# One fp32 copy of p for all batches, and a new order of all steps, in a fused attention and token-mixing kernel

## The chip, the cores and the metric

The kernel runs on one core of a Trainium2 chip. The metric is the device time of one execution in microseconds (us). Before the change three runs gave 105.6, 106.25 and 106.4 us; the median is 106.25 us. One execution was also taken with the hardware profiler: 105.87 us of device time, of which 103.7 us are the span that the trace covers.

Engines: PE is TensorE (PEld its weight loads), DVE is VectorE, ACT is ScalarE, POOL is GpSimd, SP is SyncE, which here only issues transfers. A transfer that POOL issues is a software transfer (it can convert fp32 to bf16 on the way); one that SP or ACT issues is a hardware transfer (no conversion).

## The reference

Eight batches, eight heads, 576 rows, 64 columns per head, 32 pack rows.

```python
def sm_attn(qq, kk, vv):                 # softmax(qq kk^T / 8) vv
    ...
p_packed = sm_attn(p, k, v)              # 32 rows per head
out = sm_attn(q, p_packed, p_packed)     # 576 rows per head
x = out.transpose(0, 2, 1, 3).reshape(B, S, H * D)      # 576 x 512 per batch
wq, wk = x @ w_q, x @ w_k                                # 576 x 64 each
W_tok = scale * einsum('bsd,btd->bst', wq, wk)
mixed = einsum('bst,btd->bsd', W_tok, x)
return maximum(mixed, 0) @ w_out                         # 576 x 512 per batch
```

q, k and v are 9.4 MB each in fp32, p is 0.52 MB, w_out 1.05 MB, w_q and w_k 0.13 MB each, and the output is 9.4 MB.

## The kernel before

The kernel is one list of steps, ORDER (lines 12 to 56), worked through from left to right. Each word is one step: a name, its batch and part, `@` the engine, and `=` the PSUM banks. Every engine takes its own steps strictly in this order, so the list sets the order on PE, DVE, ACT, POOL and SP alike, and a step that waits holds all later ones of its engine. Nothing is rescheduled.

Per batch the steps are these. LD.k, LD.v, LD.q load k, v and q through POOL's software queue as bf16 into four rotating buffers each. KT transposes k on DVE in blocks (line 242 is the helper of all DVE transposes). S1 is the first score product on PE. X1 is its exponential on ACT. For batches 2 to 7 TE turns the result on DVE. PV is the product with v. RC and PP divide, on DVE; PT transposes the packed rows. QK multiplies them with w_k and w_q; QKE and QD copy that out of PSUM. QV transposes q on DVE. S2 is the second score product, in two or three parts, X2 its exponential on ACT, RS the row sums and RR the reciprocals on DVE (for batch 5 HA on POOL adds halves first, line 394). AM multiplies by the reciprocals, on DVE or POOL (line 411). AT transposes that on PE, AE copies it out. WKQ, WE, GM, GE, Y, YE, MX and MR are the token mixing, RL, RLR and RLF the ReLU copies, OT and OH the product with w_out (lines 546 and 583), OE, OEF, OEH its copies out of PSUM. ST, STF and STH store the output. LD.O loads w_out; LD.W0 and LD.W1 load w_k and w_q.

WARM steps (line 621) are matmuls on zeros. Their count is in units of 128 columns. They take PE's place in line like any other step.

HOLD.v7 (line 578) is a tiny transfer on SP's queue that reads the last v buffer. It waits until v of batch 7 has landed, and SP's stores stand behind it.

The software queue keeps at most eight transfers open: each load waits until the eighth one before it has landed (v of one batch counts as two).

The start works like this. For batches 0 and 1 (DIAG, line 9), S1 takes a block-diagonal copy of p, `pblk`, as its moving operand. Its source is loaded by itself: LD.E0 and LD.E1 (line 164) bring p of batches 0 and 1 in fp32 by hardware transfers, in pieces of 64 numbers, into `p32`; EC casts them on ACT, EX transposes them in blocks on DVE into `pe`, and four PB copies on DVE put the blocks into `pblk` (line 259). LD.H on SP's queue brings the first half of k of batch 0 in fp32, which HC casts on ACT; LD.g on POOL's queue brings the other half as bf16. p of all batches comes a second time: LD.P3, P2, P1 and P0 (line 160) are four software transfers of 32 rows each into `pbf`, and PX (line 254) transposes all of it into `pT` in one DVE instruction. S1 of batches 2 to 7 takes p from `pT`.

Of the kernel before, what the change touches and what calls it, by code (L numbers as in the profile page):

```python
# [22 lines left out]
RR.1.0@V WARM.7=0 PV.2.0=0,1 PV.2.1 RL.0.1@A RS.1.2@V AM.1.0@V QD.1@A MR.0=6,7 RLR.0@A LD.k4 RR.1.2@V
MX.0.0=2,3 LD.q3 RC.2@V AT.1.0=4 AM.1.2@V AT.1.2=5 AE.1.2@A RL.0.0@A PP.2.1@V AM.1.1@P AT.1.1=6 AE.1.1@A
PP.2.0@V AE.1.0@V WARM.2=7 WKQ.1.0=0,1 WKQ.1.2 WARM.2=7 WKQ.1.1 QV.2.2@V WE.1.0@A PT.2@V S2.2.3=4,5 S2.2.2=2,3
KT.3.2@V WE.1.1@A GM.1=7 QK.2=6 GE.1@V WARM.3=0 Y.1=0,1 X2.2.2@A QKE.2@V S1.3=2,3,6,7 X2.2.3@A RS.2.4@V
RR.2.4@V LD.v4 X1.3.1@A TE.3.1@V X1.3.0@A TE.3.0@V OT.0.0=4,5 OT.0.1 LD.q4 YE.1@A AM.2.2@V OT.0.2=6,7 OE.0.0@V
OT.0.3 MR.1=2,3 OE.0.1@A RLR.1@V MX.1.1=0,1 PV.3.0=4,5 PV.3.1 RL.1.1@A RC.3@V PP.3.1@V PP.3.0@V KT.4.2@V
AM.2.3@P QD.2@P AT.2.3=2 AE.2.3@A OT.1.4=3 MX.1.0=6,7 AT.2.2=5 OEF.1.4@A AE.2.2@V WKQ.2.0=0,1 PT.3@V QV.3.2@V
WKQ.2.1 RL.1.0@A WKQ.2.2 WE.2.2@A S1.4=2,3,4,5 X1.4.1@A X1.4.0@A TE.4.1@V OT.1.0=6,7 LD.k5 GM.2=0 QK.3=1  # L30
QKE.3@A S2.3.2=4,5 X2.3.2@A S2.3.3=2,3 X2.3.3@A GE.2@V Y.2=0,1 OT.1.1 OE.1.0@A TE.4.0@V YE.2@V PV.4.0=4,5
PV.4.1 MX.2.0=0,1 RL.2.0@A RS.3.4@V LD.v5 RR.3.4@V RC.4@V LD.q5 PP.4.1@V PP.4.0@V PT.4@V OT.1.2=2,3 OT.1.3
QK.4=6 QV.4.2@V MX.2.1=0,1 MR.2=4,5 OE.1.1@A RL.2.1@A RLR.2@V AM.3.3@P QKE.4@V AT.3.3=7 AE.3.3@V QD.3@P
S2.4.2=2,3 X2.4.2@A LD.k6 KT.5.2@V S2.4.3=4,5 OT.2.2=0,1 X2.4.3@A QD.4@V RS.4.4@V RR.4.4@V AM.3.2@P AT.3.2=6
WKQ.3.0=2,3 WKQ.3.1 AE.3.2@A LD.v6 WKQ.3.2 WE.3.2@A S1.5=4,5,6,7 OT.2.3 X1.5.1@A TE.5.1@V GM.3=2 GE.3@V
OT.2.0=6,7 LD.q6 X1.5.0@A Y.3=4,5 TE.5.0@V PV.5.0=2,3 PV.5.1 OE.2.1@A YE.3@V MX.3.0=0,1 AM.4.2@P RC.5@V
PP.5.0@V AM.4.3@P PP.5.1@V RL.3.0@A MX.3.1=4,5 RL.3.1@V LD.k7 QV.5.2@V OT.2.1 OE.2.0@A LD.v7 AT.4.2=2 AE.4.2@A
# [5 lines left out]
OE.3.1@A ST.3.1 OT.4.1 OE.4.0@A QK.6=6 QKE.6@A S1.7=2,3,0,1 RS.6.4@V AM.5.3@P AT.5.3=7 OT.4.2=4,5 AM.5.2@P
QD.5@P RR.6.4@V X1.7.1@A ST.3.4 X1.7.0@A AE.5.3@V TE.7.0@V AT.5.2=6 AE.5.2@A AM.6.3@P QD.6@P TE.7.1@V ST.2.0@P
WKQ.5.0=0,1 WKQ.5.1 WKQ.5.2 WE.5.2@A OT.4.3 OE.4.1@A ST.4.1 AT.6.3=7 QV.7.1@V AE.6.3@V GM.5=2 PV.7.0=0,1
PV.7.1 QV.7.0@V AM.6.2@P GE.5@A Y.5=4,5 RC.7@V AT.6.2=3 PP.7.0@V ST.1.0 WKQ.6.0=6,7 WKQ.6.1 AE.6.2@A YE.5@A
PP.7.1@V PT.7@V WKQ.6.2 MR.5=2,3 ST.3.0 MX.5.1=4,5 RLR.5@V WE.6.2@A RL.5.1@V S2.7.0=0,1 X2.7.0@A MX.5.0=2,3
# [607 lines left out]
```

## Time and profile before

| what | value |
|---|---|
| runs | 105.6, 106.25, 106.4 us |
| profiled execution | 105.87 us, span 103.7 us |
| PE busy | 97.0 us, of which line 621 (WARM) 23.75 us |
| DVE, ACT, POOL busy | 75.7, 66.2, 49.5 us |
| read from and written to memory | 30.28 MB and 9.44 MB |
| first S1, batch 0 | 8.29 us |
| first product with w_out | 38.45 us |
| v of batch 7 landed (HOLD goes) | 76.25 us |
| last matmul ends | 99.46 us |

The profile page gives busy time per engine, the span in 40 slices, the DMA queues, the chain of work that ended last, and the costliest groups. The timeline lists instructions of one engine in order of time: start, length, engine, line, operation, operands, and in brackets the idle time before it with what released it. GB/s counts bytes written, so a load that converts fp32 to bf16 reads twice what it shows.

### The profile page before, as it was taken

To read this page: it belongs to the slowest core of one execution; us is meant where nothing else is said; L and a number is where in the kernel's file an instruction comes from. 1 tells how busy PE (TensorE), PEld (TensorE's weight loads), DVE (VectorE), ACT (ScalarE), POOL (GpSimd) and SP (SyncE) were. 2 spreads that over 40 slices of the span, in tenths; PEclk is the share of its full clock that TensorE was granted. 3 is DMA by queue.
4 is the path that set the end of the run, shared out by engine and by line. 5 is a ranking of instruction groups with operands and counts; after the bars stand their busy time and mean duration, and the time that the engine had idled before them with its cause. 6 is when DMAs were issued, how large, how long until landed. Compare 5 with 4: busy or idle time off the path is not lost.

```text
span 103.7 us, 3603 instructions
## 1 busy us (share of the span) xinstructions
PE 97.0 (94%) x1544; PEld 58.6 (57%) x1544; DVE 75.7 (73%) x151; ACT 66.2 (64%) x109; POOL 49.5 (48%) x75
## 2 busy tenths in 40 slices
PE   5999999999999999799999999999999999999930
PEld 3897645666656644456546655683567654744420
DVE  5090382969899799798699979989988998616210
ACT  5243104246896864779869869898997796658430
POOL 5999372952163326920059599405689038000000
PEclk9999999999999999999999999999999999999996
DMA  3999999999999999999999999999999999999883
GB/s 108 238 180 186 202 210 200 211 210 212 209 211 209 206 208 214 212 210 205 213 212 207 216 208 207 215 210 205 210 251 344 396 398 400 402 409 403 330 315 115
DMA packets 14079, 25.16 MB, mean 243 GB/s; under 512 B 2160, under 2 KB 7024, under 8 KB 14064
## 3 DMA queue, kind: packets, MB, share of 16 engines
q0 software_dynamic: 10448, 16.88, 84.7%
q1 hardware_dynamic: 3200, 7.87, 19.9%
q8 instruction: 12, 0.20, 0.7%
q10 hardware_dynamic: 416, 0.20, 0.7%
q14 instruction: 3, 0.02, 0.1%
HBM read 30.28 MB, written 9.44 MB: 383 GB/s over the span
## 4 chain that ended last, share of the span: by engine, by line
PE 81%; DVE 9%; ACT 3%; POOL 2%; issue 1%; DVEq 0%; POOLq 0%; ACTq 0%
PE ps L546 25%; PE ps L621 19%; PE ps L321 6%; PE ps L379 5%; PE ps L452 4%; PE ps L498 3%; PE ps L425 3%; DVE rs L400 3%; PE ps L447 3%; PE ps L473 3%; PE ps L278 2%; PE ps L342 2%; PE ps L288 2%; POOL a L411 2%; DVE a L411 2%; ACT e L384 2%
## 5 line engine op out<-in xcount | busy, mean ns | idle before, releaser
L546 PE MATMUL ps<-wout,relu 128*128 128x512 bf16 x124 | 30.5, 380 | 0.0
L621 PE MATMUL ps<-o 128*128 128x128 f32 (+3 forms) x76 | 23.7, 455 | 1.3 <-DVE o L134 1.2
L411 POOL TENSOR_TENSOR a<-e,rr 128x1024 bf16<-128x1024 f32 (+2 forms) x13 | 15.6, 1212 | 19.1 <-DVE rr L405 10.5
L127 ACT ACTIVATE o<-ps 128x1024 f32<-128x1024 f32 (+2 forms) x17 | 15.0, 888 | 7.0 <-PE ps L546 6.4
L546 PEld LDWEIGHTS <-relu 128*128 128x128 bf16 x124 | 10.7, 98 | 12.4 <-issue 1.8
L621 PEld LDWEIGHTS ps<-o 128*128 128x128 f32 x76 | 12.9, 224 | 7.2 <-issue 4.9
L384 ACT ACTIVATE e<-ps 128x256 f32<-128x256 f32 (+2 forms) x19 | 11.3, 621 | 6.0 <-PE ps L379 5.6
L509 ACT ACTIVATE relu<-ps 128x1024 bf16<-128x1024 f32 (+1 forms) x14 | 12.7, 932 | 2.2 <-PE ps L498 1.1
L176 POOL DMA_DIRECT2D v_sb<-in_v_dram x16 | 10.1, 636 | 7.3 <-DMA q_sb<-in_q_dram 2.1
L242 DVE STREAM_TRANSPOSE kT<-k_sb 128x1152 uint32<-128x1152 uint32 (+1 forms) x9 | 11.0, 1225 | 3.0 <-DMA k_sb<-in_k_dram 3.0
L242 DVE STREAM_TRANSPOSE qT<-q_sb 128x1152 uint32<-128x1152 uint32 (+1 forms) x10 | 11.2, 1121 | 0.4 <-DMA q_sb<-in_q_dram 0.3
L400 DVE TENSOR_REDUCE rs<-e 128x16 f32<-128x512 f32 (+2 forms) x13 | 10.9, 845 | 0.4 <-ACT e L384 0.4
L321 PE MATMUL ps<-v_sb,e 64*64 64x192 bf16 x288 | 7.6, 245 | 0.6 <-DVE o L131 0.6
L299 ACT ACTIVATE e1T<-ps 128x576 bf16<-128x576 f32 x12 | 7.2, 662 | 1.3 <-PE ps L288 1.2
L127 ACT ACTIVATE aT<-ps 128x128 bf16<-128x128 f32 (+2 forms) x11 | 5.3, 506 | 3.5 <-PE ps L425 2.1
L321 PEld LDWEIGHTS <-e 64*64 64x64 bf16 x288 | 6.1, 106 | 2.5 <-issue 0.8
L127 ACT ACTIVATE wkq<-ps 128x448 bf16<-128x448 f32 (+1 forms) x9 | 6.3, 713 | 1.7 <-PE ps L452 1.4
L452 PE MATMUL ps<-aT,pqk 128*128 128x256 bf16 (+1 forms) x48 | 6.8, 246 | 0.1
L379 PEld LDWEIGHTS <-qT 64*128 64x128 bf16 x320 | 5.5, 94 | 2.3 <-issue 0.7
L379 PE MATMUL ps<-ppT,qT 64*128 64x64 bf16 x320 | 6.6, 190 | 0.0
L179 POOL DMA_DIRECT2D k_sb<-in_k_dram x7 | 5.2, 743 | 3.0 <-ACT pqk L127 3.0
L447 PE MATMUL ps<-pqk,aT 128*128 128x64 bf16 x80 | 6.1, 194 | 0.1
(79 smaller groups left out, 142.8 us busy)
## 6 DMA issues: line engine op xcount, KB each, us to landing
v_sb<-in_v_dram POOLq DMA_DIRECT2D x16, 288.0 KB, 11.9
out_dram<-o SPq DMA_DIRECT2D x9, 512.0 KB, 6.9
k_sb<-in_k_dram POOLq DMA_DIRECT2D x7, 576.0 KB, 12.1
q_sb<-in_q_dram POOLq DMA_DIRECT2D x6, 576.0 KB, 15.3
out_dram<-o POOLq DMA_DIRECT2D x4, 512.0 KB, 7.6
out_dram<-o SPq DMA_DIRECT2D x5, 256.0 KB, 3.3
q_sb<-in_q_dram POOLq DMA_DIRECT2D x4, 288.0 KB, 11.1
out_dram<-orem SPq DMA_DIRECT2D x4, 256.0 KB, 5.6
```

Source lines behind the costliest of these rows:

```text
L127: nc.scalar.activation(o, i, COPY)
L176: nc.gpsimd.dma_start(v_bufs[b % NL][halves(i), 0:7:2], src)
L242: nc.vector.transpose(o, i)
L321: nc.tensor.matmul(T["pv", b][halves(cc), i], lhsT, rhs, start=n == 0, stop=n == R - 1, skip_group_check=True)
L379: nc.tensor.matmul(ps[:, y, t - t0, i], lhsT, rhs, start=e == 0, stop=e == 1)
L384: nc.scalar.activation(e2[:, t0:t1].rearrange("a t (i y n) -> a y (t i) n", i=2, y=2), T["s2", b, c].rearrange("a y t i n -> a y (t i) n") ...
L400: nc.vector.tensor_reduce(rs[:, t0 * H:t1 * H], src, axis=AX, op=ADD)
L411: e.tensor_tensor(a2[:, t0:t1].rearrange("a t i (u l) -> a (t i u) l", l=L), e2v(b, c), T["rr", b][:, t0 * H:t1 * H].to_broadcast((P, (t1 ...
L452: nc.tensor.matmul(o, pqk[:, i, Dl:], aT[:, i, c0:c1], start=i == 0, stop=i == 1)
L509: nc.scalar.activation(o, i, RELU)
L546: nc.tensor.matmul(ps, lhsT, wout[:, j, :], start=j == 0, stop=j == NJ - 1)
L621: nc.tensor.matmul(bank(int(bk), [w]), warm[:, 0:P], rhs, start=True, stop=True)
```

## The change

p is loaded once. LD.N0 (on ACT's queue) and LD.N1 (on SP's, behind LD.H) bring half of the heads each, for all batches, in fp32, into `p32`. NC.0 on ACT and NC.1 on DVE cast them to bf16. PX is split in two halves, and now runs before the first S1. PB copies the blocks for batches 0 and 1 out of `pT`. LD.E0, E1, P0 to P3, EC and EX are gone. ORDER is new from end to end, on every engine.

```diff
 ORDER = """
-SET.warm@V SET.v0@V SET.pz0@V LD.E0@A SET.tab@A SET.aT1@V LD.H@S LD.P3 LD.E1@S EC@A EX@V PB.0.1@V LD.g0
-HC@A PB.0.3@V PB.0.2@V PB.0.0@V KT.0.0@V KT.0.1@V LD.v0 WARM.4=0 WARM.16.128=0 S1.0=0,1,2 X1.0.0@A WARM.6=3
-PV.0.0=4,5 PV.0.1 RC.0@V LD.q0 LD.P2 LD.r0 LD.W0 SET.mask@P LD.k1 SET.idf@V SET.aT0@V QV.0.1@V PP.0.0@V PP.0.1@V PT.0@V
-SET.v2@V QV.0.0@V WARM.15=3 S2.0.2=6,7 LD.W1 SET.v3@P SET.aT2@V LD.P1 KT.1.2@V S2.0.1=0,1 X2.0.1@A RS.0.1@V
-SET.v1@P S2.0.0=2,3 X2.0.0@A LD.v1 LD.P0 WARM.8=4 QK.0=4 RR.0.1@V AM.0.1@V QKE.0@A LD.q1 RS.0.0@V SET.aff@P
-SET.idb@V WARM.3=5 S1.1=0,1,2 X1.1.0@A WARM.6=5 PV.1.0=4,5 PV.1.1 X2.0.2@A RR.0.0@V AT.0.1=3 AM.0.0@V AT.0.0=2
...
-AT.4.3=3 AE.4.3@A LD.r7 OT.3.0=0,1 MR.3=4,5 RLR.3@A LD.q7 OT.3.1 KT.6.2@V OE.3.0@A WKQ.4.0=6,7 WKQ.4.1 PT.5@V
...
+LD.H@S SET.warm@V SET.v0@V SET.pz0@V SET.aT0@V SET.aT1@V SET.aT2@V SET.idf@V LD.N0@A LD.N1@S SET.tab@A LD.g0
+LD.v0 LD.r0 LD.q0 LD.k1 LD.W1 LD.W0 NC.0@A NC.1@V PX.1@V PX.0@V PB.0.0@V PB.0.1@V HC@A PB.0.2@A PB.0.3@A
+KT.0.0@V KT.0.1@V SET.mask@P SET.aff@P SET.idb@V WARM.4=0 WARM.17.128=0 S1.0=0,1,2 X1.0.0@A WARM.6=3
+PV.0.0=4,5 PV.0.1 RC.0@V PP.0.1@V PP.0.0@V QV.0.0@V PT.0@V QV.0.1@V WARM.12=3 S2.0.2=6,7 X2.0.2@A RS.0.2@V
+RR.0.2@V SET.v1@P S2.0.0=0,1 LD.v1 SET.v2@P LD.q1 X2.0.0@A LD.k2 AM.0.2@P LD.v2 RS.0.0@V S2.0.1=2,3 X2.0.1@A
+WARM.6=5 AT.0.2=5 AE.0.2@A WARM.2=4 QK.0=4 RR.0.0@V AM.0.0@P KT.1.2@V QKE.0@A WARM.1=6 S1.1=0,1,2 X1.1.0@A
+RS.0.1@V RR.0.1@V AM.0.1@P QD.0@P AT.0.0=6 LD.q2 WARM.2=7 AT.0.1=7 PV.1.0=4,5 LD.k3 AE.0.0@V PV.1.1 RC.1@V
+WKQ.0.0=0,1 AE.0.1@A WKQ.0.2 PP.1.0@V WE.0.0@A PP.1.1@V PT.1@V WKQ.0.1 WE.0.1@A WARM.3=3 GM.0=3 GE.0@A QK.1=6
...
+QKE.2@A QV.2.2@V S2.2.2=2,3 GE.1@A X2.2.2@A Y.1=4,5 YE.1@A S2.2.3=6,7 QD.2@P X2.2.3@A MX.1.1=0,1 KT.3.2@V
+MR.1=2,3 RLR.1@A MX.1.0=4,5 RS.2.4@V RL.1.0@A WARM.1=6 S1.3=6,7,2,3 X1.3.0@A X1.3.1@A RR.2.4@V OT.0.0=4,5
...
+S2.5.3=6,7 Y.4=4,5 QK.5=3 YE.4@V PV.6.0=0,1 QKE.5@V PV.6.1 RC.6@V PP.6.0@V X2.5.3@A MR.4=6,7 HA.5@P PP.6.1@V
+RLR.4@A LD.q7 MX.4.0=4,5 LD.r7 RL.4.0@A PT.6@V MX.4.1=2,3 RL.4.1@A ST.0.0@P HOLD.v7 QV.6.2@V RS.5.4@V RR.5.4@V
...
-        elif a == "P":
-            c = int(b)
-            src = p.rearrange("b (i c) (y l) d -> c (b i) y (l d)", i=2, y=2)
-            nc.gpsimd.dma_start(pbf[quarter(c)], src[c])
-        elif a == "E":
-            b = int(b)
-            src = p[b].rearrange("(i c) l d -> (c l) i d", i=2)
-            (nc.sync if eng == "S" else nc.scalar).dma_start(p32[:, 2 * b:2 * b + 2], src)
+        elif a == "N":
+            i, n = int(b), L * Dh // 4
+            src = p.rearrange("b (i c) (z l) d -> i (c z) b (l d)", i=2, z=4)
+            (nc.sync if eng == "S" else nc.scalar).dma_start(p32[:, i * n:(i + 1) * n], src[i])
...
-    def EC(eng, bk):
-        copy(eng, pbe, p32.rearrange("a u d -> a (u d)"))
+    def NC(x, eng, bk):
+        n = L * Dh // 4
+        copy(eng, pbf[:, x * n:(x + 1) * n], p32[:, x * n:(x + 1) * n])
...
-    def EX(eng, bk):
-        blocks(pe.rearrange("a u l e -> a (u l e)").bitcast(u32), pbe.bitcast(u32))
-
-    def PX(eng, bk):
-        blocks(pT.rearrange("a u (y l) e -> a (u y l e)", y=2).bitcast(u32).rearrange("a (u l) -> a l u", l=L // 2),
-               pbf.bitcast(u32).rearrange("a (l n) -> a l n", l=L // 2))
+    def PX(x, eng, bk):
+        blocks(pT.rearrange("a u l e -> a (u l e)").bitcast(u32)
+               .rearrange("a (b i z l) -> a i l z b", b=B, i=2, z=4)[:, x],
+               pbf.bitcast(u32).rearrange("a (i l z b) -> a i l z b", i=2, b=B, z=4)[:, x])
 
     def PB(n, c, eng, bk):
         us = slice(0, 2 * ND)
-        copy(eng, pblk[quarter(c), us, c], pe[quarter(c), us])
+        copy(eng, pblk[quarter(c), us, c], pT[quarter(c), us])
```

Some counts of the two lists. WARM: 82 units before, 68 after; without the two steps ahead of the first S1, 62 and 47. AM: 13 of 19 steps on POOL before, 18 of 19 after (on DVE stood AM.0.0, 0.1, 0.2, 1.0, 1.2 and 2.2, and now only AM.6.3). Ahead of the first product with w_out, OT.0.0, the new list has MX.1.1, MX.1.0 and MR.1, which stood behind it. LD.q7 and LD.r7 stand behind HA.5 on POOL; before, they stood ahead of it.

More of the change, by code (lines that the diff above doesn't have):

```diff
@@ L23 @@
[L23 to L37, printed above, removed]
@@ L43 @@
[L43 to L47, printed above, removed]
@@ new lines @@
+OT.0.2=2,3 OT.0.3 WE.2.2@A GM.2=6 OE.0.1@A LD.q4 S1.4=0,1,4,5 GE.2@V QV.3.2@V QK.3=7 QKE.3@V X1.4.1@A X1.4.0@A
+OT.1.4=6 Y.2=2,3 S2.3.2=4,5 S2.3.3=0,1 YE.2@V MR.2=2,3 OEF.1.4@A X2.3.2@A LD.k5 LD.v5 MX.2.0=6,7 X2.3.3@A
+RLR.2@A RL.2.0@A OT.1.2=4,5 MX.2.1=0,1 RL.2.1@A LD.k6 TE.4.0@V TE.4.1@V PV.4.0=2,3 PV.4.1 OT.1.3 RS.3.4@V
+RR.3.4@V OT.2.2=6,7 QD.3@P OT.2.3 RC.4@V PP.4.0@V PP.4.1@V LD.q5 OE.1.1@A PT.4@V AM.3.3@P AT.3.3=0 OE.2.1@A
+AM.3.2@P AT.3.2=1 QV.4.2@V S2.4.2=2,3 X2.4.2@A S2.4.3=4,5 AE.3.3@V WKQ.3.0=6,7 AE.3.2@A WKQ.3.2 X2.4.3@A
@@ L56 @@
+STF.7.0 OH.7.0=2 OEH.7.0@V STH.7.1@A STH.7.0
 """
```

47 lines of the change are left out of this document (27 added, 20 removed).

## The prediction

> **What bounds the kernel now.** The page comes first: the busy line, the slices of DMA, the bytes, the chain that ended last.
>
> ```profile
> span 103.7 us, 3603 instructions
> PE 97.0 (94%) x1544; PEld 58.6 (57%) x1544; DVE 75.7 (73%) x151; ACT 66.2 (64%) x109; POOL 49.5 (48%) x75
> ...
> DMA  3999999999999999999999999999999999999883
> GB/s 108 238 180 186 202 210 200 211 210 212 209 211 209 206 208 214 212 210 205 213 212 207 216 208 207 215 210 205 210 251 344 396 398 400 402 409 403 330 315 115
> ...
> HBM read 30.28 MB, written 9.44 MB: 383 GB/s over the span
> ...
> PE 81%; DVE 9%; ACT 3%; POOL 2%; issue 1%; DVEq 0%; POOLq 0%; ACTq 0%
> PE ps L546 25%; PE ps L621 19%; PE ps L321 6%; PE ps L379 5%; PE ps L452 4%; PE ps L498 3%; PE ps L425 3%; DVE rs L400 3%; PE ps L447 3%; PE ps L473 3%; PE ps L278 2%; PE ps L342 2%; PE ps L288 2%; POOL a L411 2%; DVE a L411 2%; ACT e L384 2%
> ```
>
> Two resources are near their end at once. DMA is full from the second slice to the 37th: loads at about 210 GB/s written, which is 0.42 MB read per us since loads halve the bytes, then stores at 400. And PE is busy for 94%, but line 621, the zeros, holds 19% of the chain. The table by stretches says where (line 621 alone, then PE alone; the columns are length, PE busy, clock, DMA).
>
> ```profile
> 8.30:38.45 30.15, 16.64 (x43) 6.93 (x42) 1.00 1.16 206
> ...
> 55.00:99.50 44.50, 44.45 (x740) 1.00 1.05 296
> ```
>
> Up to 38.45 more than half of PE's time is filler: data arrives too slowly for real work. From 55 on PE has real work without a gap. So there are two stages. The first goes by arrivals, and what counts is how much real PE work is behind PE when w_out arrives. The second is a backlog: what was done earlier comes off the end, one to one, until DMA's own end stops it.
>
> The arrivals are read from the timeline of DVE and PE and from the waits.
>
> ```profile
> 17.56 1.38 DVE L242 STREAM_TRANSPOSE kT<-k_sb 128x1152 uint32<-128x1152 uint32 x1 [2.17 <-DMA k_sb<-in_k_dram]
> 27.55 1.38 DVE L242 STREAM_TRANSPOSE kT<-k_sb 128x1152 uint32<-128x1152 uint32 x1 [0.27 <-DMA k_sb<-in_k_dram]
> 35.83 1.38 DVE L242 STREAM_TRANSPOSE kT<-k_sb 128x1152 uint32<-128x1152 uint32 x1 [0.55 <-DMA k_sb<-in_k_dram]
> ...
> 19.17 1.24 PE L278 MATMUL ps<-o,kT 128*64 128x128 bf16 x36
> 28.98 0.51 PE L288 MATMUL ps<-kT,pT 32*32 32x288 bf16 x32
> 37.93 0.49 PE L288 MATMUL ps<-kT,pT 32*32 32x288 bf16 x32
> ...
> PEld L546 <- DMA wout<-in_moe_w_out_dram: 0.3, 1, 0.3
> ```
>
> k of batches 1, 2 and 3 lands at 17.5, 27.5 and 35.8; S1.1, S1.2 and S1.3 follow at 19.17, 28.98 and 37.93. w_out lands just before 38.45 (PE's weight load waits 0.3 us for it).
>
> **The change part by part.**
>
> *Bytes.* Before, p is read as 4 x 0.131 MB in software transfers plus 0.131 MB for E0 and E1; after, 0.524 MB once. Saved: 0.131 MB / 0.42 = 0.31 us of DMA. Ahead of k1 nothing changes: E, P3, P2 and W0 (0.524 MB) give way to N0 and N1 (0.524 MB). So k1 stays at 17.5, and from q1 on every arrival is 0.3 us earlier.
>
> *The head.* Timelines of ACT, DVE and PE, then the DMA list:
>
> ```profile
> 4.80 0.42 ACT L127 ACTIVATE o<-o 128x256 bf16<-128x256 f32 x1 [2.06 <-DMA o<-in_p_dram]
> ...
> 5.25 0.31 DVE L242 STREAM_TRANSPOSE o<-o 128x128 uint32<-128x128 uint32 x1 [2.89 <-ACT o L127]
> 5.60 1.09 DVE L131 COPY o<-o 32x256 bf16<-32x256 bf16 x4
> 6.61 1.42 DVE L242 STREAM_TRANSPOSE kT<-k_sb 128x576 uint32<-128x576 uint32 x2
> ...
> 8.29 1.25 PE L278 MATMUL ps<-o,kT 128*64 128x128 bf16 x36
> ...
> o<-in_p_dram ACTq DMA_DIRECT2D x1, 64.0 KB, 3.8
> o<-in_p_dram SPq DMA_DIRECT2D x1, 64.0 KB, 3.5
> ...
> L242 DVE STREAM_TRANSPOSE pT<-o 128x512 uint32<-128x512 uint32 x1 | 1.0, 1005 | 0.0
> L207 DVE CAST idb<-o 128x128 bf16<-128x128 f32 x1 | 0.2, 215 | 0.0
> L131 DVE COPY o<-ps 128x512 f32<-128x512 f32 x1 | 0.7, 691 | 0.1
> ```
>
> Before, EX starts 0.5 us after E1 has landed (4.7), and DVE works 0.31 + 1.09 + 1.42 us to the first S1. After, DVE does NC.1, two PX halves, two PB and two KT. NC.1, a 128x512 cast, lies between the 0.215 us of a quarter of its width and the 0.69 us of a copy of its size out of PSUM: 0.5. PX halves: 1.005 in all. PB: 0.55 (the other two go to ACT). That is 2.05 ahead of KT against 1.40, +0.65 us; but DVE starts on landing, no longer behind EC. When N1 lands is unknown: it is 262 KB instead of 66, behind the same LD.H.
>
> ```profile
> 3.00:3.50 0.50, 0.50 (x4) 0.44 (x3) 0.00 (x0) 0.00 (x0) 0.50 (x2) 1.00 1.10 421
> ...
> 4.50:5.00 0.50, 0.50 (x5) 0.50 (x4) 0.00 (x0) 0.20 (x1) 0.50 (x2) 1.00 0.99 137
> ```
>
> N0 and N1 are 0.39 MB more than E0 and E1 on the hardware queues: at 421 GB/s 0.9 us more, at the mean of these two rows (279) 1.4 us. The other end is no loss: the last E bytes drip in at 137 GB/s with DMA full, so their short pieces may cost as much time as N's longer ones. So N1 lands at 4.7 to 6.1; I take 5.3, nearer to the measured row. S1.0 then starts at 8.29 + 0.65 + 0.1 (= 5.3 + 0.05 - 5.25) = 9.0, bounds 8.4 to 9.8.
>
> The Trainium skill, "DMA: Bandwidth & Descriptors", Specifications, has a rule here: pieces under 512 bytes are read, modified and written back. E's pieces are 64 fp32 numbers, 256 bytes, and N's 2 KB; the slow 4.50:5.00 row agrees, and by the rule S1.0 would be near 8.4.
>
> *What hides a late S1.0.* From S1.0 to S1.1 the old list took 19.17 - 8.29 = 10.9 us, with 32 units of filler; the new one has 27. A unit is 16.64 / 62 = 0.27 us by the row above, or 0.20 by the chain (19% of 103.7 less the 7.2 us ahead of S1.0, over 62). So the new stretch needs about 9.8 us with AT.0.2 added: 18.8 from 9.0, and k1 with its transpose holds S1.1 to 19.0 anyway. Cover for 0.2 us; at 9.8 S1.1 would be 0.6 late, and the next gate, k2, takes that back, since the new list has another 10 units less up to w_out.
>
> *AM on POOL.* DVE loses six AM and gains one.
>
> ```profile
> L411 POOL TENSOR_TENSOR a<-e,rr 128x512 bf16<-128x512 f32 x3 | 3.1, 1041 | 4.5 <-DVE rr L405 4.0 <-DMA v_sb<-in_v_dram 0.6
> L411 DVE TENSOR_TENSOR a<-e,rr 128x512 bf16<-128x512 f32 x3 | 2.1, 687 | 0.1
> ```
>
> Each is 0.35 us longer on POOL, and loads stand behind it. LD.q2 is behind all three AM of batch 0, the last of which waits for RR.0.1, and that for k1's transpose (18.9) and a row sum on DVE: issued at about 22, by my estimate. What is queued ahead of it, through v2, is 3.54 MB for each of batches 0 and 1, k2 and v2 (2.36), p (0.52) and the small weights (0.26), 10.2 MB; done by 22 are (22 - 2.3) x 0.42 = 8.3, DMA having begun at 2.3. That leaves 1.9 MB, 4.5 us of cover: DMA doesn't notice. AT.0.1 is ready at about 21.5, when PE is through S1.1 and its filler: no loss.
>
> *Work moved ahead of w_out.* MX.1.1, MX.1.0 and MR.1 now run before OT.0.0. A piece of the chain in order of time shows one MX:
>
> ```profile
> 29.48 0.33 PE ps L498 x2
> ```
>
> Two of these are 0.66 us; with MR.1's four small matmuls I take 0.7. S1.3 needs k3 at 35.5 plus 1.4: 37.1; OT.0.0 then waits for w_out, 38.45 - 0.3 = 38.1. The work left at 38.1 is 0.7 us shorter, the start 0.3 earlier: a lead of 1.0 us (0.3 if the moved work finds no room, 1.6 if both AT.2 also get ahead of PV.3, as listed).
>
> *The end.* Stretches, then the last copy and its store:
>
> ```profile
> 95.00:97.50 2.50, 2.50 (x13) 1.14 (x12) 1.41 (x3) 1.26 (x3) 0.00 (x0) 1.00 0.90 346
> 97.50:100.00 2.50, 1.95 (x14) 1.08 (x11) 0.42 (x1) 1.58 (x3) 0.00 (x0) 1.00 0.89 333
> 100.00:103.70 3.70, 0.00 (x0) 0.00 (x0) 0.00 (x0) 0.00 (x0) 0.00 (x0) 0.76 0.50 177
> ...
> 99.49 0.39 ACT L127 ACTIVATE o<-ps 128x256 f32<-128x256 f32 x1 [0.28 <-PE ps L583]
> 99.55 0.63 ACTq L592 DMA_DIRECT2D out_dram<-o  x1
> ```
>
> After 95 the stores write 0.87 + 0.83 + 0.65 = 2.35 MB in 8.7 us; at 403 GB/s they need 5.8. But the last stretch must keep its shape, since the last store can start no sooner than the last copy: its 177 GB/s are 1.6 us of bytes in 3.7, so about 2 us of it move none. So DMA lets the end come 2.9 - 2 = 0.9 us earlier, plus the 0.3 of the bytes: 1.2 at most. The lead of 1.0 nearly fits: **-0.9 us**.
>
> The sum: 105.87 - 0.9 = 104.97. The profiled execution is 0.4 us under the median; I forecast 105.0, faster by 1.2%.
>
> **The rivals.**
>
> *Only the bytes come off* (106.0). The lead is lost at a later gate, such as k7, which lands only 0.3 us earlier, or DMA's end holds. For it: DMA full in 35 slices. Against: the dip of the last three slices.
>
> *q7 and r7 come late* (slower). They now stand behind HA.5 on POOL.
>
> ```profile
> 64.12 1.14 POOL L182 DMA_DIRECT2D q_sb<-in_q_dram  x2
> ...
> 69.96 1.55 POOL L394 TENSOR_TENSOR h<-e 128x640 f32<-128x640 f32 x1 [3.88 <-ACT e L384]
> ...
> 76.25 0.64 SPq L578 DMA_DIRECT2D touch<-v_sb  x1
> 80.04 0.77 DVE L242 STREAM_TRANSPOSE qT<-q_sb 128x576 uint32<-128x576 uint32 x1
> ```
>
> Before, they were issued at 64.12; behind HA.5 it is 71.5, or 70.5 with the lead. v7's bytes end about 76.25 - 1.18 / 0.42 = 73.4; a load needs 2 to 3 us to begin (64 KB took 3.5 to land, 0.2 of it bytes). Issued by 71, q7 just meets the end of v7. Later, stores (released by v7) share DMA: 1.18 MB at half rate take 5.6 us instead of 2.8. From 72 on, by my estimate, each us of HA.5 delays QV.7.0, S2.7 and the end alike; 2 us late gives +1 to +2.5, 107.6. Against: X2.5.3, HA.5's input, should lead too.
>
> *N lands at 6.1 or after* with a slow cast: S1.0 at 10 or later, not all given back: 106.7.
>
> *The clock falls.* The 100.00:103.70 row shows 0.76 with PE idle; all others 1.00. With 15 units less filler PE idles, by my walk at most 0.8 us at a time. A wait long enough to halve the clock would stretch the following few us of matmuls: +1.5, 107.4. The Trainium skill, "TensorE: Matmul & The Clock Gate", Part 1, speaks against the change here: an idle window of about 3.4 us throttles. By that rule, gaps of 0.8 us do nothing.
>
> **How the numbers follow.** Forecast 0.54 (104.0 to 105.6; 0.40 of it faster by over 1%, about what a measurement here can tell), bytes only 0.20, late N 0.07 (half within 1%), late q7 and r7 0.16, clock 0.03. Faster 0.40, same 0.14 + 0.20 + 0.03 = 0.37, slower 0.23. Low end: 1.6 of lead and DMA's 1.2 give 104.3, with 0.4 for the head: 103.9. High end into the q7 rival: 107.4.
>
> **What would show it.** S1.0 near 9.0, S1.1 near 19, OT.0.0 near 38.1 with both MX.1 done; line 621 near 13 us after S1.0; PE without gaps from 43; q7 issued by 71; last matmul near 98.5. Wrong, if PE idles after 40, if QV.7.0 waits for DMA, or if DMA dips before 95.

## The result and the profile after

The changed kernel takes 110.09 us (median of five runs, 109.56 to 111.35). The kernel before, on the same chip, takes 105.73 us. The ratio is 1.038, 95% interval 1.031 to 1.045: **slower by 3.8%**, where 1% faster was forecast. The profiled execution (111.35 us) is one of two longer ones, which this ratio and those below leave out on either side, so about 1.5 us of what follows belongs to that execution.

The page after: the busy line, the slices, the bytes, the chain that ended last.

```profile
span 109.6 us, 3592 instructions
PE 97.1 (89%) x1540; PEld 59.1 (54%) x1540; DVE 72.1 (66%) x140; ACT 66.4 (61%) x111; POOL 52.9 (48%) x81
...
PEclk9999755999999999999999999999999999999997
DMA  3999999997999999999999999999699999997885
GB/s 108 273 181 197 214 203 202 215 210 106 180 184 212 185 205 215 211 205 181 209 206 213 211 207 210 181 174 202 90 145 358 411 416 414 398 405 283 328 308 177
...
HBM read 30.15 MB, written 9.44 MB: 361 GB/s over the span
...
PE 68%; DVE 9%; ACT 8%; DMA 7%; POOL 2%; issue 2%; SPq 0%; ACTq 0%; DVEq 0%
```

The bytes went down as the change says (30.28 to 30.15 MB). Three things are new: DMA has 7% of the chain, the clock drops in slices 5 to 7 (counted from 1), and DMA writes little in slices 10, 29 and 30. A piece of the chain in order of time (start, length, what) says what the 7% is:

```profile
1.18 8.11 DMA o<-in_p_dram
```

LD.N1, the second half of p, is the path for 8.1 of the first 9.3 us. The list of transfers (count, KB, us from issue to landing) sets it against the two that start beside it:

```profile
o<-in_k_dram SPq DMA_DIRECT2D x1, 576.0 KB, 4.0
...
o<-in_p_dram ACTq DMA_DIRECT2D x1, 256.0 KB, 4.5
o<-in_p_dram SPq DMA_DIRECT2D x1, 256.0 KB, 8.1
```

And the timelines of SP, DVE, PE and POOL:

```profile
1.18 0.68 SPq L160 DMA_DIRECT2D o<-in_p_dram  x1
...
9.31 0.43 DVE L131 CAST o<-o 128x512 bf16<-128x512 f32 x1 [6.64 <-DMA o<-in_p_dram]
9.77 1.09 DVE L236 STREAM_TRANSPOSE pT<-o 128x256 uint32<-128x256 uint32 x2
10.90 1.21 DVE L131 COPY o<-pT 32x256 bf16<-32x256 bf16 x2
12.15 1.44 DVE L236 STREAM_TRANSPOSE kT<-k_sb 128x576 uint32<-128x576 uint32 x2
...
12.98 0.31 PE L271 MATMUL ps<-o,kT 128*64 128x128 bf16 x1 [4.78 <-DVE kT L236]
13.64 2.13 PE L271 MATMUL ps<-o,kT 128*64 128x128 bf16 x35 [0.35 <-DVE kT L236]
...
26.15 1.24 PE L271 MATMUL ps<-o,kT 128*64 128x128 bf16 x36
...
45.05 1.89 PE L539 MATMUL ps<-wout,relu 128*128 128x512 bf16 x8 [0.29 <-ACT relu L502]
...
104.70 1.04 PE L576 MATMUL ps<-wout,relu 128*128 128x256 bf16 x8
...
24.04 0.61 POOL L404 TENSOR_TENSOR a<-e,rr 128x256 bf16<-128x256 f32 x1 [9.73 <-DVE rr L398]
...
28.18 0.77 POOL L181 DMA_DIRECT2D q_sb<-in_q_dram  x1
```

DVE sits for 6.6 us until LD.N1 has landed at 9.3. PE runs out of zeros and idles for 4.8 us. The first S1 starts at 12.98 (before: 8.29), the second at 26.15 (19.17), OT.0.0 at 45.05 (38.45), and the last matmul ends at 105.74 (99.46).

Five differences account for the whole time. The columns are the start of the first S1, from there to the second S1, from there to OT.0.0, from there to the last matmul's end, and the rest (to the end of the run).

| kernel | S1.0 | to S1.1 | to OT.0.0 | to the last matmul | rest | sum |
|---|---|---|---|---|---|---|
| before | 8.29 | 10.88 | 19.28 | 61.01 | 6.41 | 105.87 |
| after | 12.98 | 13.17 | 18.90 | 60.69 | 5.61 | 111.35 |
| difference | +4.69 | +2.29 | -0.38 | -0.32 | -0.80 | +5.48 |

All of the loss lies ahead of the second S1. Behind it the new order is 1.5 us shorter than the old one.

### The profile page after: what moved, and what is told of

The parts are those of the page before. It is cut to its first block, busy times and chain, and to the rows that moved or that the text cites. A ratio compares the mean times of both kernels' runs of the same rounds, so it can differ in the third digit from the quotient of the medians.

```text
span 109.6 us, 3592 instructions
## 1 busy us (share of the span) xinstructions
PE 97.1 (89%) x1540; PEld 59.1 (54%) x1540; DVE 72.1 (66%) x140; ACT 66.4 (61%) x111; POOL 52.9 (48%) x81
## 2 busy tenths in 40 slices
DMA packets 13567, 25.29 MB, mean 231 GB/s; under 512 B 1584, under 2 KB 6448, under 8 KB 13552
## 3 DMA queue, kind: packets, MB, share of 16 engines
q1 hardware_dynamic: 3072, 8.32, 19.7%
HBM read 30.15 MB, written 9.44 MB: 361 GB/s over the span
## 4 chain that ended last, share of the span: by engine, by line
PE 68%; DVE 9%; ACT 8%; DMA 7%; POOL 2%; issue 2%; SPq 0%; ACTq 0%; DVEq 0%
PE ps L539 25%; PE ps L614 11%; DMA o<-in_p_dram 7%; PE ps L314 6%; PE ps L372 4%; PE ps L418 3%; PE ps L271 3%; PE ps L445 3%; ACT relu L502 3%; DVE kT L236 2%; PE ps L440 2%; POOL a L404 2%; DVE o L131 2%; PE ps L335 2%; ACT e L377 2%; PE ps L491 2%
## 5 line engine op out<-in xcount | busy, mean ns | idle before, releaser
L404 POOL TENSOR_TENSOR a<-e,rr 128x256 bf16<-128x256 f32 (+2 forms) x18 | 19.6, 1098 | 22.9 <-DVE rr L398 16.9
L539 PE MATMUL ps<-wout,relu 128*128 128x512 bf16 x124 | 30.0, 380 | 0.3 <-ACT relu L502 0.3
L614 PE MATMUL ps<-o 128*128 128x128 f32 (+3 forms) x72 | 21.8, 444 | 1.9 <-DVE o L134 1.2
L127 ACT ACTIVATE o<-ps 128x1024 f32<-128x1024 f32 (+1 forms) x16 | 14.7, 919 | 7.7 <-PE ps L539 7.4
L614 PEld LDWEIGHTS ps<-o 128*128 128x128 f32 x72 | 12.1, 226 | 7.3 <-issue 4.4
L502 ACT ACTIVATE relu<-ps 128x1024 bf16<-128x1024 f32 (+1 forms) x13 | 12.2, 968 | 0.4 <-PE ps L491 0.4
L127 ACT ACTIVATE wkq<-ps 128x448 bf16<-128x448 f32 (+1 forms) x10 | 7.2, 728 | 3.0 <-PE ps L445 1.5
L271 PE MATMUL ps<-o,kT 128*64 128x128 bf16 x72 | 3.7, 264 | 5.1 <-DVE kT L236 5.1
L318 DVE RECIPROCAL rec<-ps 128x2 f32<-128x2 f32 x8 | 1.3, 160 | 10.2 <-PE ps L314 10.2
L129 POOL COPY pqk<-pqk 128x128 bf16<-128x128 bf16 x8 | 2.4, 296 | 10.3 <-DVE pqk L131 6.9
```

What stands on the lines that cost most here:

```text
L127: nc.scalar.activation(o, i, COPY)
L404: e.tensor_tensor(a2[:, t0:t1].rearrange("a t i (u l) -> a (t i u) l", l=L), e2v(b, c), T["rr", b][:, t0 * H:t1 * H].to_broadcast((P, (t1 ...
L502: nc.scalar.activation(o, i, RELU)
L539: nc.tensor.matmul(ps, lhsT, wout[:, j, :], start=j == 0, stop=j == NJ - 1)
L614: nc.tensor.matmul(bank(int(bk), [w]), warm[:, 0:P], rhs, start=True, stop=True)
```

## The experiments

The table gathers what most of the runs below turn on: when the last part of p that the first S1 needs has landed (issue plus landing time), the starts of the steps, and the ratio to the kernel before. In the column on the shape, 16 x 8 is the nested shape of the change, and 128 rows a shape that is explained further on.

| kernel | order, shape of p | p landed | S1.0 | S1.1 | OT.0.0 | ratio (95% interval) |
|---|---|---|---|---|---|---|
| new_order_e | new, old loads | 4.8 | 8.19 | 20.15 | 39.06 | 1.001 (0.998 to 1.004) |
| old_order_n | old, 16 x 8 | 9.4 | 12.69 | 25.67 | 44.85 | 1.057 (1.051 to 1.063) |
| after | new, 16 x 8 | 9.3 | 12.98 | 26.15 | 45.05 | 1.038 (1.031 to 1.045) |
| n1_first | new, 16 x 8, N1 ahead of H | 5.5 | 10.17 | 20.75 | 39.66 | 1.004 (0.999 to 1.009) |
| n_128_rows | new, 128 rows | 6.0 | 9.37 | 19.98 | 38.89 | 0.992 (0.990 to 0.994), from n_128_rows_t |
| n_rows_right_ha | new, 128 rows | 5.6 | 8.76 | 19.41 | 38.32 | 0.989 (0.985 to 0.993) |

### Which half of the change costs the time

First the change was cut in two: the old list with the new loads, and the new list with the old loads.

```diff
# old_order_n
-LD.E0@A ... LD.P3 LD.E1@S EC@A EX@V ... LD.P2 ... LD.P1 ... LD.P0 ... PX@V
+LD.N0@A ... LD.N1@S NC.0@A NC.1@V PX.1@V PX.0@V ...
# new_order_e
-LD.H@S ... LD.N0@A LD.N1@S SET.tab@A LD.g0 LD.v0 LD.r0 LD.q0 ... NC.0@A NC.1@V PX.1@V PX.0@V PB ...
+LD.E0@A SET.tab@A ... LD.H@S LD.P3 LD.E1@S ... EC@A EX@V PB.0.1@V LD.g0 LD.v0 LD.r0 LD.P2 LD.q0 ...
+LD.P1 and LD.P0 ahead of LD.v1 and LD.q1, PX@V behind QV.1.2
```

> The old order with the new load alone: N0 and N1 in the places of E0 and E1, two NC and two PX in the places of EC and EX, P0 to P3 and the late PX gone. If the new load is the cause, the first S1 starts at 12 us or later and the time is 109 to 111. If the new order is the cause, the time is 106 to 107.

> The new order with the old loads: E0, E1, P0 to P3, EC, EX, PX as before, all else in the changed kernel's order. If the new load is the cause of the loss, the first S1 starts at 8.3 to 8.8 us and the time is 104.5 to 105.5, as the prediction had it. If the new order carries part of it (AM and HA.5 ahead of loads on POOL), DMA dips stay and the time is 106 to 108.

Measured: 1.057 and 1.001. The loads alone cost more than the whole change; the order alone costs nothing, and gains nothing either. In the old order too LD.N1 takes 8.2 us to land.

### Where in SP's queue LD.N1 stands

```diff
# n1_first
-LD.H@S ... LD.N0@A LD.N1@S
+LD.N1@S LD.H@S ... LD.N0@A
# n1_on_act
-LD.N0@A LD.N1@S
+LD.N0@A LD.N1@A
```

> The changed kernel with LD.N1 ahead of LD.H on SP's queue. Theory A (N1 was late because it stood behind 590 KB of H on its queue): N1 lands by 5.5 us, H by 7, the first S1 starts near 9.5, and the time comes back to about 106. Theory B (any hardware transfer that is still under way when the software queue is filled gets only a part of the DMA time, whichever it is): N1 lands by 5.5 but H now lands at 9 or later, the first S1 stays at 12 to 13 us and the time at 109 to 110. Theory C (the shape with 16 outer rows is slow by itself): N1 still takes 8 us.

Measured: 1.004. LD.N1 lands in 4.8 us, by 5.5, and now LD.H takes 6.6, so the first S1 waits for ACT, which stands in H's cast, until 10.17. That is 2.8 us sooner than after, and in the profiled execution (105.67 us) enough to bring the time back to that of before. It isn't in every one: the median of the ten runs is 107.43 us, and in five of them the mean clock is 0.984 instead of 0.99 to 1.00.

> The changed kernel with LD.N1 issued from ACT behind LD.N0, so that LD.H has SP's queue to itself. Theory A (a hardware transfer that stands behind another one on its queue is left to compete with the software queue, and gets about a third of the DMA time): H lands at 4.7 as in the changed kernel, N1, behind only 262 KB, lands near 6.5, the first S1 starts at 10 to 10.5, the time is 105.5 to 106.5. Theory C (the shape is slow by itself): N1 lands at 8 or later and the time stays above 108.

Measured: 1.045 (1.038 to 1.052). LD.H gets faster (3.7 us), but the two p transfers take 6.1 us in the median and the second lands at 9.0, so the first S1 starts at 12.76. The expectation of 6.5 was wrong: what LD.N1 waits for isn't LD.H in its queue.

### The clock and the zeros

```diff
# fill_head
-WARM.17.128=0
+WARM.44.128=0
# no_mid_fill: fill_head, and between S1.0 and S1.1
-WARM.6=3 ... WARM.12=3 ... WARM.6=5 ... WARM.2=4 ... WARM.1=6
# no_late_fill: fill_head, and the 20 units behind S1.1 left out
```

> The changed kernel with 44 instead of 17 units of filler ahead of the first S1, so that PE has no idle stretch there. If the fallen clock carries part of the loss, the first S1 stays near 13 to 13.5 us, the granted clock stays at 1.00, S1.1 comes 1.5 to 2 us earlier than at 26.15, and the time is 1 to 2 us under that of the changed kernel (108 to 109). If the late landing alone carries it, the time stays at 110.

Measured: 1.048 (1.043 to 1.053). The clock stays at 1.00 through the whole profiled execution (109.51 us), and from S1.0 to S1.1 it needs 9.98 us instead of 13.17. But S1.0 itself now stands behind 27 more units and starts at 14.05. Between the two profiled executions that comes to 1.8 us less (111.35 and 109.51); the medians (110.09 and 110.81 us) show no gain. Keeping the clock up with zeros doesn't bring the time back, since the zeros that do it stand ahead of S1.0.

> As the run with 44 units ahead of the first S1, but without the five pieces of filler (27 units) between S1.0 and S1.1. Theory F (the filler turns what would be slack into work, so that a late start is passed on): S1.1 starts near 19.5 to 20.5 instead of 24.0, and the time falls by 3 to 4 us, to 106 to 107. Rival (the steps behind S1.0 wait for data or for POOL anyway): S1.1 stays after 23 and the time at 109 to 111.

Measured: 1.047 (1.038 to 1.056). The timelines show why zeros between S1.0 and S1.1 don't matter:

```profile
20.69 0.42 DVE L390 TENSOR_REDUCE rs<-e 128x8 f32<-128x256 f32 x1 [0.80 <-ACT e L374]
21.14 0.20 DVE L395 RECIPROCAL rr<-rs 128x8 f32<-128x8 f32 x1
21.33 0.69 DVE L390 TENSOR_REDUCE rs<-e 128x16 f32<-128x512 f32 x1
22.05 0.25 DVE L395 RECIPROCAL rr<-rs 128x16 f32<-128x16 f32 x1
22.22 1.32 DVE L233 STREAM_TRANSPOSE kT<-k_sb 128x1152 uint32<-128x1152 uint32 x1
...
23.59 2.13 PE L268 MATMUL ps<-o,kT 128*64 128x128 bf16 x36 [0.57 <-DVE kT L233]
```

KT.1.2, which S1.1 needs, stands on DVE behind RS.0.0 and RR.0.0 of batch 0. The second S1 therefore comes 9.6 us behind the first even with no zeros between them: the softmax of batch 0 is the distance.

> As the run with 44 units of filler ahead of the first S1, but without the eight pieces (20 units) behind S1.1. If these pieces keep a late start from being made good while the data is there, the first product with w_out comes 2 to 4 us earlier than in that run and the time falls to 106 to 108. If the steps wait for each other anyway, it stays at 109 to 111, as it did without the pieces ahead of S1.1.

Measured: 1.044 (1.039 to 1.050). Without zeros behind S1.1 PE waits instead for AM on POOL (1.06 and 0.80 us), X2 on ACT and the first ReLU, and OT.0.0 starts at 43.45, 0.5 us later than in fill_head (42.94), which has these zeros. The clock falls here and in no_mid_fill too, so these two runs bound the zeros' share only roughly; neither gets near 38.5.

### HA.5 and the loads of q7

```diff
# ha_behind_q7
-HA.5@P ... LD.q7 ... LD.r7
+LD.q7 ... LD.r7 HA.5@P
```

> The changed kernel with HA.5 moved behind LD.q7 and LD.r7 on POOL. If the DMA dip of the slices 28 and 29 (90 and 145 GB/s) is a cost of its own, the dip fills and the time falls by 1 to 2 us, to 108 to 109. If it only reflects that PE is late anyway, the dip goes and the time stays at 110.

Measured: 1.045 (1.038 to 1.053), no gain. q7 is issued at 70.50 instead of 77.23, the two low slices (29 and 30 counted from 1; the expectation counts from 0) fill from 90 and 145 to 199 and 244 GB/s, and the time stays. So with the whole kernel late they are no cause of it.

> The new order with the old loads, and AM.0.2 ahead of LD.k2 on POOL, since LD.k2 there waits for k1, which it doesn't in the changed kernel. If the new order is worth the 0.9 us of the prediction once the loads are in time, S1.1 starts at 19.1 to 19.4 instead of 20.2, OT.0.0 near 38.2, and the time is 104.7 to 105.2. If the lead is lost in other waits, the time stays within 0.5% of the kernel before.

```diff
# new_order_e2: new_order_e, and
-LD.k2 AM.0.2@P
+AM.0.2@P LD.k2
# new_order_e2ha: new_order_e2, and HA.5@P behind LD.r7
```

> As the run with AM.0.2 ahead of LD.k2, with HA.5 also behind LD.q7 and LD.r7. If q7 and r7 behind HA.5 cost DMA time at the end of the loads, the time falls by another 0.3 to 0.8 us; if not, it is the same.

Measured: 0.998 (0.994 to 1.001) and 0.994 (0.990 to 0.997). In new_order_e2 S1.1 starts at 18.94, as hoped, but OT.0.0 only at 38.63: the lead is lost in between. In a kernel that is in time, moving HA.5 may be worth some 0.4%; the intervals overlap. In n1_first no gain shows (1.0039, and 1.0041 with the move), but the intervals, 0.999 to 1.009 and 1.001 to 1.007, are too wide to exclude 0.4%:

> Edit: the kernel after with LD.N1 ahead of LD.H on SP's queue, and HA.5 behind LD.r7 on POOL. Theory: with the head 2.5 us earlier than in the kernel after, q7 and r7 are worth the 0.4% that they were worth in the timely kernel with the old loads: ratio 0.997 to 1.003 against the kernel before, no dip of DMA in slices 28 and 29. Rival: as in the late kernel the move gives nothing: 1.003 to 1.008.

### The software queue

> The changed kernel with four of POOL's memsets ahead of LD.g, so that the software queue starts about 2.4 us later. Theory A/B (N1 loses to the software queue): N1 lands at 5.5 to 6.5 instead of 9.3. Theory C (16 outer rows are slow by themselves, or H ahead of it on the queue is all that counts): N1 still lands at 8 or later. The time itself says little, since k, v and q of batch 0 are also later.

```diff
# g_late
-LD.g0 ... SET.mask@P ... SET.v1@P ... SET.v2@P ... SET.v3@P
+SET.mask@P SET.v1@P SET.v2@P SET.v3@P LD.g0
# e_g_first: new_order_e, and
-LD.P3 ... LD.g0 LD.v0 LD.r0 ... LD.q0
+LD.g0 LD.v0 LD.r0 LD.q0 LD.P3
```

Measured, in one execution: 106.45 us. With the software queue begun 2 us later (LD.g at 3.24 instead of 1.27), LD.N1 lands in 5.1 us instead of 8.1 and the first S1 starts at 9.35. So what LD.N1 loses time to are the software transfers, as far as one execution can tell.

> The new order with the old loads, and the software queue filled as in the changed kernel: LD.g, v0, r0 and q0 ahead of LD.P3. If what starves a hardware transfer is that the software queue has filled by then, E1 (66 KB, behind H) lands at 6 us or later instead of 4.8. If it is N1's size, E1 stays below 5.3 us.

Measured, in one execution: 109.42 us, but not by a late p: LD.E1 lands in 3.6 us as ever and the first S1 starts at 8.12. The loss comes later (second S1 at 22.70; on POOL LD.k2 waits 2.83 us for a load of k to land, and AM.0.2 stands behind it). So a filled software queue doesn't slow every hardware transfer. What is it about LD.N1: its 256 KB, or its shape?

### The shape of the transfer

LD.N1 reads 16 outer rows (four heads by four quarters of a head) with eight batches inside each, in pieces of 2 KB. The same pieces can be named as 128 rows with one stride:

```diff
# n_128_rows, n_128_rows_t
-src = p.rearrange("b (i c) (z l) d -> i (c z) b (l d)", i=2, z=4)
+src = p.rearrange("(i b) h (z l) d -> i (b h z) (l d)", i=2, z=4)
```

> Edit: the two p transfers are cut as 128 rows of 2 KB with one stride each (four batches per transfer) instead of 16 outer rows by 8 batches; same bytes, same queues, same place. This puts p's rows in other places than the kernel after, so what is computed is not the reference; all work stays. Theory size: a 262 KB hardware transfer that runs beside the filled software queue gets a small share, whatever its shape: LD.N1 still takes 7.4 to 8.2 us to land, the first S1 starts at 12.7 to 14, time 109 to 112. Rival shape: the 16 outer rows are what is slow: LD.N1 lands in 6 us or less, the first S1 at 11 or earlier, time 106 to 107.

> Edit: none against n_128_rows; the same kernel, timed (p's rows still lie in other places than in the kernel after, all work stays). Theory shape, after one look at 104.86 us with LD.N1 landing by 5.9: the interval of the ratio lies below 1, near 0.991 to 0.995, and LD.N1 lands by 6.3 in the profiled execution. Rival: that one execution was chance, and LD.N1 lands now early and now late: median between 105.5 and 109.5 with a wide spread.

Measured: one execution of 104.86 us, then 0.992 (0.990 to 0.994). **The shape decides** when LD.N1 lands; the theory of size falls. Shape here means two things that no run separates: the nesting, and the places in memory, since the 128 rows lie in one block of 256 KB, while the nested transfer steps 64 KB from one piece to the next. And the nested shape is not slow by itself: LD.N0 has it too, on ACT's queue, and lands in 4.5 us after, where the 128 rows take 4.7. The list of transfers of n_128_rows, to set beside that of after:

```profile
o<-in_k_dram SPq DMA_DIRECT2D x1, 576.0 KB, 4.6
...
o<-in_p_dram ACTq DMA_DIRECT2D x1, 256.0 KB, 4.7
o<-in_p_dram SPq DMA_DIRECT2D x1, 256.0 KB, 4.8
```

Its timelines of SP, DVE, PE and POOL:

```profile
1.19 0.42 SPq L160 DMA_DIRECT2D o<-in_p_dram  x1
...
5.97 0.43 DVE L131 CAST o<-o 128x512 bf16<-128x512 f32 x1 [3.30 <-DMA o<-in_p_dram]
...
9.37 0.25 PE L271 MATMUL ps<-o,kT 128*64 128x128 bf16 x1 [1.33 <-DVE kT L236]
...
19.98 1.24 PE L271 MATMUL ps<-o,kT 128*64 128x128 bf16 x36
...
38.89 1.89 PE L539 MATMUL ps<-wout,relu 128*128 128x512 bf16 x7 [0.29 <-ACT relu L502]
...
22.01 0.77 POOL L181 DMA_DIRECT2D q_sb<-in_q_dram  x1
...
70.71 1.12 POOL L178 DMA_DIRECT2D q_sb<-in_q_dram  x2
```

Two more views tell how the two shapes differ. The stretches (last two columns: DMA's share, GB/s written) of the kernel after, then of n_128_rows:

```profile
4.00:5.00 1.00, 1.00 (x7) 1.00 (x7) 0.00 (x0) 0.00 (x0) 1.00 (x2) 1.00 0.93 182
...
4.00:5.00 1.00, 1.00 (x7) 1.00 (x7) 0.00 (x0) 0.00 (x0) 1.00 (x2) 1.00 1.00 391
...
11.00:15.00 4.00, 4.00 (x53) 2.23 (x48) 1.28 (x4) 1.13 (x1) 0.95 (x2) 1.00 1.11 211
```

The DMA view by queue, for one window each (packets, MB, share of the 16 DMA engines' time; a packet in this view is one piece). q0 is the software queue, q1 is SP's and q10 ACT's. The kernel after, from 0 to 4 us, then from 4 to 9 us:

```profile
q1 hardware_dynamic: 144, 0.59, 41.9%
...
q0 software_dynamic: 393, 0.57, 78.7%
q1 hardware_dynamic: 144, 0.26, 15.8%
```

n_128_rows, from 0 to 5 us, then from 5 to 6 us:

```profile
q1 hardware_dynamic: 202, 0.71, 39.3%
q10 hardware_dynamic: 144, 0.26, 17.7%
...
q0 software_dynamic: 63, 0.15, 75.5%
q1 hardware_dynamic: 86, 0.14, 37.6%
```

LD.H is 0.59 MB and LD.N1 0.26 MB. In the kernel after, SP's queue is through with LD.H by 4 us; all of LD.N1 comes later, between 4 and 9 us, with 15.8% of DMA's time beside software transfers with 78.7%. In n_128_rows no software packet starts before 5 us, and by 6 us SP's queue has moved both its transfers. So there the hardware transfers are nearly through before the software ones begin, although LD.g is issued at 1.27 in both kernels.

The issue itself differs too: LD.N1's takes 0.68 us on SP after and 0.42 in n_128_rows (the first lines of the two timelines). All loads of p in the nested shape take 0.64 to 0.72 us to issue; the other loads that SP and ACT issue at the start, LD.E's of before among them, 0.38 to 0.47, except that LD.H takes 0.8 where it stands behind LD.N1 (n1_first).

Why the software packets begin later in n_128_rows isn't shown. It is not the size of the pieces: both pages have 3072 on SP's queue and the same counts by size (1584 under 512 B, 6448 under 2 KB, 13552 under 8 KB). The Trainium skill, "DMA: Bandwidth & Descriptors", Queues, rings and completion order, says that each DMA engine goes round between the queues that have work, packet by packet, where a packet holds several pieces. That would fit how LD.N1 shares DMA once the software queue runs; how the pieces were bundled no run here shows.

The next try kept the nesting and took the second half of p off the path, by cutting p by batches:

```diff
# n_by_batch (and n_by_batch_ha, with HA.5@P behind LD.r7)
-src = p.rearrange("b (i c) (z l) d -> i (c z) b (l d)", i=2, z=4)
+src = p.rearrange("(x b) (i c) (z l) d -> x i (c z) b (l d)", x=2, i=2, z=8)
+two transfers of 128 KB for each of LD.N0 and LD.N1; NC.0@V PX.0@V ahead of PB, NC.1@V PX.1@V behind KT.0.1
```

> Edit: p is cut by batches instead of by heads: LD.N0 (ACT's queue) brings batches 0 to 3 and LD.N1 (SP's, behind LD.H) batches 4 to 7, each as two transfers of 32 outer rows by 4 batches in pieces of 1 KB; NC.0 and PX.0 on DVE are all that PB and the first S1 need, NC.1 and PX.1 stand on DVE behind KT.0.1. What is computed is the reference. Theory: the first S1 no longer hangs on what stands behind LD.H, so it starts at 8.5 to 10 even where LD.N1 lands at 8 or 9; time 104.7 to 105.8, ratio 0.990 to 1.000. Rival: transfers in few outer rows or short pieces are slow wherever they stand, or delay LD.H: the first S1 at 11 or later, time 106 or more.

> Edit: n_by_batch with HA.5 behind LD.r7 on POOL. Theory: in a kernel whose head is in time, q7 and r7 ahead of HA.5 are worth 0.4%, as from new_order_e2 to new_order_e2ha: ratio about 0.004 below that of n_by_batch. Rival: nothing, as from n1_first to n1_first_ha (1.0039 and 1.0041).

Measured: 1.018 (1.014 to 1.022) for the first, whose six runs spread from 107.40 to 110.80 us (median 108.94); those of the second spread from 107.11 to 111.45 us (median 109.89) and say nothing on HA.5. The rival held: the two halves of LD.N0 take 5.3 us in the median and DVE gets them at 8.25, so the first S1 starts at 10.69. Here even 128 KB in nested shape are late, while LD.H beside them lands in 3.6 us.

### A version that beats both

In n_128_rows p's rows lie in other places. The last run brings them to the right ones:

```diff
# n_rows_right_ha: loads of n_128_rows, HA.5@P behind LD.r7, and
-PX.1@V PX.0@V PB (from pT)
+PX.0@V PB (from a tile pX that PX writes) ... NC.1@V PX.1@V behind SET.idb
+PC.2.0 to PC.2.3@V behind PX.1, PC.3 and PC.0@A behind X1.0.0, PC.1@P behind LD.k2: copies from pX to pT
```

> Edit: p loaded as in n_128_rows (128 rows of 2 KB, one stride), and p's rows now brought to their places: PX writes to a tile of its own (batch by batch on the partitions), PB takes its blocks from there, and 16 new copies PC move the other batches to pT, on DVE, ACT and POOL in their gaps before 17 us; NC.1 and PX.1 stand behind KT.0.1; HA.5 stands behind LD.r7. What is computed is the reference. Theory: the shape decides, so LD.N0 and LD.N1 land by 6.3, the first S1 starts at 9 to 10.3, the copies cost nothing, ratio 0.987 to 0.995 against the kernel before. Rival: what the row order saves in the load is paid back by the copies: the first S1 at 10.5 or later or DVE late for RC.0, ratio 0.996 to 1.01.

Measured: 104.37 us, 0.989 (0.985 to 0.993), 1.1% faster than the kernel before and so faster than both kernels. Its timelines of PE and ACT:

```profile
8.76 0.25 PE L275 MATMUL ps<-o,kT 128*64 128x128 bf16 x1
...
19.41 1.24 PE L275 MATMUL ps<-o,kT 128*64 128x128 bf16 x36
...
38.32 1.89 PE L543 MATMUL ps<-wout,relu 128*128 128x512 bf16 x7 [0.29 <-ACT relu L506]
...
11.85 2.96 ACT L125 ACTIVATE pT<-o 32x256 bf16<-32x256 bf16 x8
16.05 1.36 ACT L381 ACTIVATE e<-ps 128x256 f32<-128x256 f32 x3 [1.24 <-PE ps L376]
```

PE has no idle time ahead of the first S1, and the copies on ACT end 1.2 us before X2 wants it. From S1.0 to S1.1 it takes 10.65 us, against 10.61 in n_128_rows without the copies, so they cost next to nothing.

## Why the prediction was wrong

**The head: the step that failed.** "N lands at 4.7 to 6.1; I take 5.3" was worked out from bytes at 279 to 421 GB/s, as if the hardware queues came first. LD.N1 landed at 9.3, 3.2 us beyond the upper end, since its 0.26 MB had 15.8% of DMA from 4 to 9 us. The bytes were right: in 128 rows the same 256 KB, behind the same LD.H, land by 5.97, where their cast starts, inside the range. What failed is the silent step that a transfer's shape doesn't count once its pieces are long. It counts here because the software queue runs beside it: started 2 us later, it lets the nested transfer land in 5.1 us (g_late). Why the shape matters to the queue stays open.

One of its rows was misread as well. "The last E bytes drip in at 137 GB/s" is about the 4.50:5.00 row of before; by queue, software transfers have that window to themselves:

```profile
q0 software_dynamic: 31, 0.07, 99.0%
```

E's last bytes were through before, so the mean of 279 GB/s, and with it the bound of 6.1, has no ground in that row, and the row doesn't bear out the rule that was cited beside it. That rule of the Trainium skill ("DMA: Bandwidth & Descriptors", Specifications), on pieces under 512 bytes, was taken to put the first S1 at 8.4 with N's longer pieces. The runs went the other way: E's 64 KB in 256-byte pieces landed in 3.5 to 4.0 us, LD.N1's 256 KB in 2 KB pieces in 8.1. Nothing here shows that rule at fault; it is not what decides.

The rest of the head held. From the cast to the first S1 the forecast has 3.7 us (5.3 to 9.0); n_128_rows needs 3.4 (5.97 to 9.37), after 3.7. S1.0 of n_128_rows is at 9.37, within the bounds of 8.4 to 9.8. Two errors cancel in it: the two PB copies on DVE take 0.91 us there and 1.21 after, where 0.55 was set, and S1.0 starts on the first half of KT instead of behind both.

**"What hides a late S1.0": the second step that failed.** It said that k1 holds S1.1 to 19.0 anyway and that k2 takes the rest back. Neither is so. From S1.0 to S1.1 the new list takes 10.6 us at full clock in n1_first, n_128_rows and n_rows_right_ha, where 9.8 was set, since KT.1.2 stands behind batch 0's softmax; in n_128_rows it starts at 18.47 without a wait for k1. In fill_head it is 9.98 only because S1.0 has no gap in its middle: from the end of S1.0 to S1.1 it is 8.73 us there and in n_128_rows. From S1.1 to OT.0.0 it takes 18.90 to 18.92 us in 13 of the 18 kernels with the new order, after among them, whether S1.1 starts at 19.41 or at 26.15. The 15 units less of filler did not become slack: the steps on PE follow each other without gaps, or wait for one another's results on DVE, ACT and POOL. The loads are in that line too: POOL stood 9.73 us ahead of AM.0.2 after (5.34 in n_128_rows), LD.q2 went out at 28.18 (the forecast 22; n_128_rows 22.01), and DMA fell to 106 GB/s in slice 10. Of a late S1.0 nothing is given back in these kernels, and the backlog carries it to the end.

**The rivals.** "N lands at 6.1 or after" was the case that came, with a chance of 0.07 and 106.7 us: the place right, the price 3.4 us too small because of "not all given back". "The clock falls" came too, as its consequence: PE idled for 4.8 us, not 0.8, and the clock halved. From S1.0 to S1.1 it took 13.17 us instead of 10.6, so 2.6 us, against the 1.5 set; that is part of the loss in the profiled execution, beside 3.6 us for the start itself (12.98 against 9.37). In executions of other kernels whose mean clock was 0.984 or 0.979 (n1_on_act 12.01, n_128_rows_t 12.25) it took 1.4 to 1.6 us more, so for the kernel after's runs at 0.978 to 0.984 the 1.5 may be near. "q7 and r7 come late" did not decide: moving HA.5 brought nothing in the kernel after. Its times were right where the head is in time (q7 at 70.71, forecast 70.5), and there the move may be worth 0.4 us, where +1 to +2.5 was set.

**The new order.** Forecast: 0.3 us from the bytes, 0.7 from work moved ahead of w_out, 0.9 off the end, 105.0 in all. With the head in time n_128_rows gives 104.86 us in one execution, and n_128_rows_t a median of 105.16 and a ratio of 0.992. The parts: OT.0.0 starts at 38.89, not 38.1, since it waits for the first ReLU and not for w_out; from there to the last matmul 0.68 us less than before (60.33 against 61.01), as set; the rest 0.8 less, which no term of the forecast has (0.4 of it lies outside the span of the trace: 2.17 us before, 1.8 in n_128_rows). So a gain of the size that was argued exists once p lands early, and it is in part luck that the sum agrees: one part came out worse and another better than set. With the old loads the new order alone reached 1.001. The change as made doesn't reach the gain, by the shape of one transfer.
